# Another written order for the steps of a fused delta-rule and mixer kernel

## The chip, the cores and the metric

The kernel runs on one core of one Trainium2 chip. The metric is the device time of one execution in microseconds (us), lower is better. The kernel before took 581.09, 582.49 and 582.77 us in three runs, so its median is 582.49 us.

The core has five engines, each with its own list of instructions, taken in order: PE (TensorE, the matrix engine; its weight loads are a row of their own, PEld), DVE (VectorE), ACT (ScalarE), POOL (GpSimd) and SP (SyncE, which here only issues DMAs). The program makes the engines wait for each other with semaphores.

## The reference

Two blocks follow each other. The first is a delta-rule recurrence over 4 batches and 8 heads, 768 tokens with head size 48. The second is a mixer on the result with 384 channels: a low-rank mix over the tokens, and then a two-layer channel network of width 1536.

```python
for t in range(S):
    kt, vt, bt = (k_n[:, :, t], v[:, :, t], beta[:, :, t, None])
    y[:, :, t] = np.einsum('bhd,bhde->bhe', q[:, :, t], state)
    v_old = np.einsum('bhde,bhd->bhe', state, kt)
    state = state + bt[:, :, :, None] * np.einsum('bhd,bhe->bhde', kt, vt - v_old)
...
h = xt @ U @ V
u = x + h.transpose(0, 2, 1)
ch = np.maximum(u @ w_ch1, 0.0) @ w_ch2
return (u + ch).astype(np.float32)
```

`k_n` is k divided by its norm, and `xt` is x with tokens and channels exchanged.

## The kernel before

**Work.** The recurrence is done in chunks of 64 tokens, 12 per batch. A batch is cut into two units of six chunks, so there are eight units, n = 0 to 7. For a unit, `grams` transposes k and q (`turn`, line 374) and forms products of keys with keys and of queries with keys (`products`, line 400). `blocks` (line 439) inverts the 32x32 triangles on DVE by forward substitution. For each column it multiplies into `prod` (line 468) and subtracts from `xt` (line 469). That is 15 columns for units 0 to 2, which work on half triangles, and 31 for the others. `joins` (line 501) builds the 64x64 inverses from the triangles by short alternations of PE, ACT and DVE. Then `recur` (line 599) walks the 12 chunks of a batch. For units 0 and 1 a chunk is a PE step that applies the old state (line 697), a DVE step that forms `z` (line 704), a PE step for the new state (line 714) and a DVE step that adds it up as `s` (lines 720 and 722). From unit 2 on there are three PE steps: line 673, then `rest` on DVE (line 679), line 686, then `z` on ACT (line 689), line 714, then `s` on DVE. `outputs` (line 614) computes y of a chunk, and `put` copies it to `X` with ACT.

**Weights.** The weights arrive as 64-bit numbers. `load_weights` (line 748) loads them in 14 slices, and converts each with three DVE steps (lines 809, 815 and 818) and one ACT step (line 796). The 14 slices are U, V, six for the first layer, six for the second.

**Mixer.** A batch has three groups of 256 tokens. `front` (line 1015) does the low-rank mix and the transposition, `channels` (line 1099) the first layer in six pieces, `narrow` (line 1178) the second layer in four. `early` (line 929) and `ahead` (line 944) do the first layer of the very first group from x before its low-rank part is there. They are the first long matmuls of the program. `ahead` needs `early`, which needs the first four chunks of batch 0 in `X`, and the first-layer weights. The last batch takes another way for the first layer (`quick`, line 866).

**Order.** No planner runs in the kernel. Each piece of work is a Python generator, a *part*, which yields one step after another. A step is a few instructions of one engine. Parts get numbers as they begin, and `ORDER` (line 52) is a list of 2342 part numbers. `run` (line 186) walks it and lets the named part emit its next step. A number behind a dot names the PSUM bank, and a q asks for the form of a mixer step that works on quarters of the matrix engine (64x64 tiles). Since each engine has its own list, a token's place matters only against other tokens of the same engine. The parts 0 to 200 begin before the first token, so they have the same numbers in every order, for instance: 4, 9, 10, 11 are `recur` of batches 0 to 3; 12 is `norms` of unit 0; 17 and 18 turn q of unit 0; 19, 34, 51, 68, 85, 102, 119, 136 are `blocks` of units 0 to 7; 23 and 24 load v of unit 0; 146 is `load_weights`, 147 to 160 the loads of its slices; 162 is `weight_sums`; 166 is `early`, 167 to 172 are `ahead`. Parts that begin later (outputs, joins, channels) have numbers that depend on the order.

```python
for token in ORDER.split():
    i, bank, quad = (token.partition('q')[0] + '.').split('.')[0], token.partition('.')[2], 'q' in token
    step = waits[int(i)]
    if isinstance(step, tuple):
        step = step[quad]
```

## Time and profile before

| what | value |
|---|---|
| runs | 581.09, 582.49, 582.77 us; median 582.49 us |
| profiled execution, first to last instruction | 581.3 us |
| PE busy | 549.3 us (94%) |
| DVE busy | 405.2 us (70%) |
| ACT busy | 248.1 us (43%) |
| mean granted PE clock | 0.988 |

The profile is of one execution, and only its span is shown, not its time with what lies around the span. The span stands 1.2 us below the median of the runs and 0.2 us above the fastest of them.

The views used are: the page's busy sums and its rows in 40 slices of 14.5 us; the table of busy time by stretch, in which each row has the stretch, its length, and for every engine busy us and number of instructions, then the granted clock, the DMA share and GB/s; the chain of work that ended last, in order of time (start, us, what); the list of who waited for whom; and the groups of instructions by line. A busy PE means only that matmuls are under way, since they overlap.

### The profile page before, as it was taken

Reading aid. Unit: us, or ns where it says so; the run is one execution under the profiler, and the core shown is the slowest. Engines: PE = TensorE matmul, PEld = TensorE weight load, DVE = VectorE, ACT = ScalarE, POOL = GpSimd, SP = SyncE. Lnnn points to the kernel's source line nnn. Section 1 sums busy time; section 2 is a strip of 40 time slices with the busy share of each in tenths; the row PEclk is TensorE's granted clock in tenths of the full one; section 3 lists DMA queues with packets and bytes.
Section 4 is the critical chain, followed back from the end, with each engine's and each line's share of the span. In section 5 each row is a group of like instructions: output and inputs, shape, how many; then the busy total and the mean of one; then the engine's idle time right before and its main releaser. Section 6 shows DMA issues by size and latency. Waiting matters only on the chain.

```text
span 581.3 us, 25150 instructions
## 1 busy us (share of the span) xinstructions
PE 549.3 (94%) x11349; PEld 464.3 (80%) x11349; DVE 405.2 (70%) x1006; ACT 248.1 (43%) x526; POOL 97.8 (17%) x169
## 2 busy tenths in 40 slices
PE   5766999999999999999999999999999999999997
PEld 4665887669889788789879876989879869656997
DVE  6999875699998239899972899998323248157442
ACT  3678886553333553254245323631531331465000
POOL 8212150260001214221014105200000000000000
PEclk9999689999999999999999999999999999999999
DMA  9997292280000243620014204200000000000010
GB/s 146 171 249 194 75 224 54 56 151 6 30 4 16 46 76 62 111 45 3 30 24 95 61 14 85 54 29 2 31 3 2 31 2 1 28 1 0 15 41 28
DMA packets 63851, 33.38 MB, mean 57 GB/s; under 512 B 50816, under 2 KB 61824, under 8 KB 63744
## 3 DMA queue, kind: packets, MB, share of 16 engines
q1 hardware_dynamic: 56800, 23.21, 18.6%
q0 software_dynamic: 5344, 8.27, 6.6%
q8 instruction: 89, 1.46, 1.1%
q10 hardware_dynamic: 1600, 0.30, 0.3%
q14 instruction: 18, 0.15, 0.1%
HBM read 27.03 MB, written 4.72 MB: 55 GB/s over the span
## 4 chain that ended last, share of the span: by engine, by line
PE 80%; DVE 14%; issue 2%; ACT 1%; DMA 1%; SPq 0%; DVEq 0%; ACTq 0%
PE P L1214 25%; PE P L1126 13%; PE P L206 10%; PE P L904 7%; PE P L407 3%; PE P L951 3%; PE P L218 2%; DVE prod L468 2%; DVE xt L469 2%; PE P L628 2%; PE P L621 2%; PE P L686 2%; PE P L923 1%; PE P L1049 1%; PE P L673 1%
## 5 line engine op out<-in xcount | busy, mean ns | idle before, releaser
L1126 PE MATMUL P<-ut,w_sb 128*128 128x256 f32 x384 | 88.4, 385 | 0.1
L1214 PE MATMUL P<-w_sb,hs 128*128 128x192 f32 x456 | 79.9, 330 | 0.5 <-issue 0.5
L1126 PEld LDWEIGHTS P<-ut,w_sb 128*128 128x128 f32 x384 | 71.3, 190 | 11.1 <-issue 1.2
L1214 PEld LDWEIGHTS P<-w_sb,hs 128*128 128x128 f32 x456 | 74.1, 190 | 2.2 <-issue 1.3
L469 DVE TENSOR_TENSOR xt<-xt,prod 128x112 f32<-128x112 f32 (+21 forms) x200 | 64.6, 323 | 6.9
L468 DVE TENSOR_TENSOR prod<-gs,xt 128x112 f32<-128x112 f32 (+21 forms) x200 | 63.5, 318 | 2.5
L1096 ACT ACTIVATE hs<-P 128x512 f32<-128x512 f32 x48 | 28.7, 597 | 66.9 <-PE P L1126 52.4
L206 PE MATMUL P<-ut,w_sb 64*64 64x256 f32 x768 | 55.9, 383 | 0.9 <-ACT hs L1096 0.6
L1160 DVE TENSOR_TENSOR X<-X,P 128x192 f32<-128x192 f32 x85 | 29.2, 347 | 38.1 <-PE P L1214 35.2
L1214 PE MATMUL P<-w_sb,S 128*128 128x192 f32 x240 | 41.6, 329 | 0.0
L1214 PEld LDWEIGHTS P<-w_sb,S 128*128 128x128 f32 x240 | 39.0, 190 | 0.4
L407 PE MATMUL P<-slot 48*64 48x64 f32 x1536 | 34.6, 244 | 4.0 <-issue 2.0
L611 ACT COPY X<-P 64x192 f32<-64x192 f32 x96 | 30.0, 312 | 15.4 <-PE P L628 13.8
L591 POOL MEMSET slot<- 32x384 f32 x32 | 13.7, 433 | 135.7 <-PE P L562 126.0
L587 ACT COPY slot<-zz 32x384 f32<-32x384 f32 x64 | 32.2, 508 | 10.2 <-DVE zz L473 8.9
L407 PEld LDWEIGHTS P<-slot 48*64 48x64 f32 x1536 | 30.9, 156 | 7.0 <-issue 3.0
L206 PEld LDWEIGHTS P<-ut,w_sb 64*64 64x64 f32 x768 | 27.3, 133 | 9.5 <-issue 2.5
L720 DVE TENSOR_TENSOR s<-s,P 128x192 f32<-128x192 f32 x40 | 14.0, 350 | 29.8 <-PE P L714 25.0
L310 POOL DMA_DIRECT2D slot<-in_q_dram x32 | 20.9, 657 | 80.9 <-DVE prod L468 31.1
L689 ACT COPY z<-P 128x192 f32<-128x192 f32 x36 | 11.4, 318 | 53.2 <-PE P L686 45.9
L310 POOL DMA_DIRECT2D slot<-in_k_dram x44 | 29.0, 667 | 22.2 <-PE P L714 17.3
L889 DVE TENSOR_TENSOR slot<-slot,P 128x384 f32<-128x384 f32 x36 | 19.4, 553 | 19.1 <-PE P L904 18.1
(182 smaller groups left out, 1048.1 us busy)
## 6 DMA issues: line engine op xcount, KB each, us to landing
w_sb<-in_moe_w_ch_dram SPq DMA_DIRECT2D x14, 384.0 KB, 4.3
out_dram<-X SPq DMA_DIRECT2D x22, 192.0 KB, 2.0
slot<-in_k_dram SPq DMA_DIRECT2D x48, 72.0 KB, 4.1
slot<-in_k_dram POOLq DMA_DIRECT2D x44, 72.0 KB, 4.3
slot<-in_q_dram SPq DMA_DIRECT2D x32, 72.0 KB, 4.8
slot<-in_q_dram POOLq DMA_DIRECT2D x32, 72.0 KB, 4.9
slot<-in_v_dram SPq DMA_DIRECT2D x32, 72.0 KB, 3.9
slot<-in_v_dram POOLq DMA_DIRECT2D x32, 72.0 KB, 3.0
```

What stands on the lines that cost most here:

```text
L206: nc.tensor.matmul(to[half(g)], w[half(r), half(g)], x[half(r)], start=start, stop=stop, skip_group_check=True)
L310: queue.dma_start(out=t[half(1 - g if name == 'z' else g), :, to, 0:D], in_=src[b, 4 * g + s, hf * UC * L:(hf + 1) * UC * L, :].rearrange( ...
L407: nc.tensor.matmul(p_g[half(g ^ par * i), par, c], kq[rows, c, j, 0, half(g)], kq[rows, c, j, i, half(g)], start=True, stop=True)
L468: nc.vector.tensor_tensor(out=prod, in0=gb[:, :, j:j + 1, j + 1:].to_broadcast([128, split, m, w]), in1=xb[:, :, 0:m, j:j + 1].to_broadcas ...
L469: nc.vector.tensor_tensor(out=xb[:, :, 0:m, j + 1:], in0=xb[:, :, 0:m, j + 1:], in1=prod, op=ALU.subtract)
L587: nc.scalar.copy(pg[quarter(i), :, at, :, a:a + BK], cut(zc, h)[quarter(i)].rearrange('p r (c j) t -> p r c j t', j=2))
L611: nc.scalar.copy(x[half(c % 2), c // 2, 4 * D * g:4 * D * (g + 1)].rearrange('p (j r d) -> p r j d', r=2, d=D), states(p_y)[half(g)])
L904: nc.tensor.matmul(banks[x], w1_sb[:, 4 * a[0] + e, a[1]] if isinstance(a, tuple) else w1_mixes[a][:, e], tokens(*t) if isinstance(t, tupl ...
L1096: nc.scalar.activation(hs[:, fs[0]:fs[1] + 1:fs[1] - fs[0]], p_f, ACTF.Relu)
L1126: nc.tensor.matmul(p_f[:, x], w(x, t), ut[:, t], start=t == 0, stop=t == KT - 1)
L1160: nc.vector.tensor_tensor(out=to, in0=to, in1=p, op=ALU.add)
L1214: nc.tensor.matmul(to, of[0], of[1], start=of[2], stop=of[3], skip_group_check=True)
```

## The change

The text of `ORDER` is replaced. Nothing else in the file differs. Each part has the same number of tokens as before where its number is fixed (0 to 200), the whole list has 2342 tokens before and after, and 25 tokens carry a q in both. So the same steps are issued on the same engines, in another sequence on each of them. A few rows of the diff, from the beginning, the start of batch 1 and the stretch with the last weight sums:

```diff
-    1 0 1 0 1 0 1 0 2 1 36 147 37 21 150 22 36 152 153 151 149 14.3 37 21 201 2 148 201 37 36 22 36 22 21 15.1
-    20 38 202.2 148 203 39 146 148 146 204 203 2 37 21 146 205.0 202 22 154 148 202 26 38 202 29.3 39 205 149
...
-    223 220 146 34 226 218 27 218 34 218 34 217 146 217 220 217 155 34 155 218.3 218 220 155 34 218 220 217
...
-    326 330 9 330 319 319 9.1 330 9 341.2 342 9.0 9 324 331q 9.1 331 9 341 343.0 331 9.1 341 331 9 324 9.1 341
...
+    1 0 0 0 0 1 14.3 1 1 15.2 147 201 150 202 201 146 204 203.1 203 202 205.0 205 37 37 146 146 203 203 36
+    205 205 2 2 2 2.3 36 2 2 2 36 36 19 20 205 12 29.2 21 206 2 12 19 19 19 37 37 30.3 19 38 38 208 39 39 19
...
+    152 24 151 212 212 34 34 34 156 216 213 213 213 24 214.3 214 214 151 26 26 214.3 214 220 220 34 34 146
...
+    9 9.2 320 68 321 318 318 318 68 291.0 291 291 9 291 68 303 306 306 68 323 9.2 326 326.1 326 9 325 328
...
+    330 9 330 342 326 326 9.0 9 61 9.0 9 331q 331 75 325 331 9.0 9 341 343.2 341 341 325 325 325 331 9.0 9
```

## The prediction

> **What bounds the kernel now.** I read the page first: busy sums and the rows in 40 slices.

> ```profile
> span 581.3 us, 25150 instructions
> ...
> PE 549.3 (94%) x11349; PEld 464.3 (80%) x11349; DVE 405.2 (70%) x1006; ACT 248.1 (43%) x526; POOL 97.8 (17%) x169
> ...
> PE   5766999999999999999999999999999999999997
> ...
> DVE  6999875699998239899972899998323248157442
> ...
> PEclk9999689999999999999999999999999999999999
> ```

> PE is at 9 everywhere but in the first four slices. An order can only win where PE has nothing to do, so I asked for the busy time by stretch, cut where the first long matmuls (`ahead`, line 951) start in the chain of waits, at 77 us. Columns: stretch, length, then busy us of PE, PEld, DVE, ACT, POOL, clock, DMA.

> ```profile
> 0.00:77.00 77.00, 55.05 (x1708) 50.05 (x1712) 66.41 (x188) 54.34 (x104) 25.15 (x46) 0.91 0.78 173
> 77.00:130.00 53.00, 51.21 (x1267) 38.35 (x1256) 38.44 (x82) 32.77 (x62) 20.99 (x34) 1.00 0.56 108
> 130.00:570.00 440.00, 435.06 (x8347) 368.16 (x8347) 298.57 (x733) 160.94 (x361) 51.66 (x89) 1.00 0.15 32
> ```

> PE idles 22.0 us before 77 us, 1.8 us from there to 130, and 4.9 us in the next 440. So there are two regimes: a start of 77 us in which PE is fed late, and then a PE that is full. What feeds it late is in the chain of the start (start us, us, what):

> ```profile
> 41.05 1.04 DVE w_sb L818
> ...
> 63.10 0.24 DVE z L704
> ...
> 66.79 0.37 DVE z L704
> ...
> 77.42 2.35 PE P L951 x10
> ```

> From 12.4 to 67 us nearly every link of this chain is DVE, and in 12 to 66.8 us DVE is busy 51.6 of 54.8 us. The link at 66.79 is z of the fourth chunk of batch 0, the last that `early` needs, and `early` opens `ahead`. So the start lasts as long as the DVE work written before that z. Part of it is weight conversion:

> ```profile
> L818 DVE SCALAR_TENSOR_TENSOR w_sb<-w_sb,X 128x768 uint16<-128x768 uint32 x7 | 7.1, 1019 | 0.0
> L809 DVE TENSOR_SCALAR power<-w_sb 128x768 int32<-128x768 int32 x7 | 4.1, 591 | 0.0
> L815 DVE TENSOR_SCALAR X<-w_sb 128x768 int32<-128x768 int32 x7 | 4.1, 589 | 0.0
> ```

> A full slice costs 1.02 + 0.59 + 0.59 = 2.2 us of DVE, and one ACT cast of 1.06 us (line 796). After 77 us the waits of PE are few and short (waited for; us in total, times, longest):

> ```profile
> PE P L621 <- DVE s L720: 1.0, 3, 0.6
> PE P L1214 <- DVE X L1160: 0.9, 2, 0.4
> ```

> **The change, part by part.** It removes and adds no instruction, so each cost is one of place. I counted tokens of parts with fixed numbers, and told later parts by their pattern of dots and counts; a step's time is its row's busy sum over its count.

> *Start, DVE.* Before, the z in question is the sixth DVE token of part 4, list place 336, and 26 tokens of part 146 (the conversions) stand ahead of it: eight slices and two steps of a ninth. After, it is at place 299 with 17 tokens ahead: five slices and two steps. The same DVE work of units 0 and 1 stands ahead in both: part 19 whole, part 34 whole, both norms, the masks. So 3 x 2.2 = 6.6 us of conversion move behind z, which comes near 60.2 us. The end of blocks 1 (last token of 34) goes from place 302 to 283 with it.

> *Start, other engines.* Ahead of the first token of 167, ACT has 90 tokens instead of 108 (four or five casts of 1.06 us, a dozen copies of 0.5 us, so about 9 us less). ACT was busy 14.2 us of 60 to 75, so it needed this relief, or it would have been the next bound. From z to `early` it took 66.8 to 74.3 us, with PE steps of 6.8 us by their rows in between; now 3.2 us of steps stand there, 3.6 less. From `early` to `ahead` it took 3.1 us with 4.6 us of steps, now 6.8, so about 1.5 more. The first `ahead` matmul moves by -6.6 - 3.6 + 1.5 = -8.7 us, to about 69. Against it: PE has done less by then. Five `joins` steps (0.64 us in the 32x32 form, 0.79 in the other, together 3.5) now stand behind. All PE groups sum to 647 us by their rows against 549 busy, since steps overlap, so this costs 3.0 us later. The moved conversions find room: DVE has 14.6 us free in 77 to 130, and the sixth first-layer slice is still converted ahead of the `ahead` step that uses it.

> *Start, DMAs.* Loads are reordered on SP and POOL. The queries of unit 0 come later (last on SP is its 22nd issue, not its 16th; turned at places 116 and 143 instead of 79 and 106), and v of unit 0 must wait for that turn. Before, v is issued from 23.0 to 28.7 us on SP, is scaled on DVE at 38.05, and lands in 3.9 us (median). After, the last turn stands behind some 24 us of DVE work, and before the z link 62 us of such work ended at 66.8, so about 5 us are to be added: it comes at about 30 us, v lands at about 38, and its scaling, with 41 us of DVE work ahead of it, is due at about 46. That leaves about 8 us, so I cost it at nothing; without that cover each us late is a us lost.

> So the start gives -8.7 + 3.0 = -5.7 us. Bounds: -1, if the alternations of `joins` (PE waits of 4.4 us at lines 525, 539 and 561 in the start) become the chain once fewer conversions stand between them, and -9, if the deferred steps find gaps of PE.

> *After the start, recurrence gaps.* Between two PE steps of a recurrence lies an eviction (0.35 us, rows of lines 720 and 679) and its hand-overs. What hides it is PE work written in between: a y step is 0.47 us (20.9 us over 44), a turn 0.66, a single `ahead` step 0.51, a quarter-array piece 0.87, another recurrence step 0.45. Before, most gaps behind the first `ahead` step hold 0.87 us or more. Five hold less: three in batch 0 and two in batch 1. If 0.9 us is the need, they miss 1.9 us in sum, and the waits of PE after 77 us that name s, z or rest or their ACT copies sum to 1.8. So I take 0.9. After, 13 hold less: four in batch 0 (missing 1.4), six in batch 1 (2.5; in the row `9.0 9 61 9.0` nothing at all stands between), two in batch 2 (0.9) and one in batch 3 (0.4). That is 5.2 instead of 1.9, +3.3 us. Bounds: 0, if the evictions come sooner, and +9, below.

> *After the start, changes of tiling.* A block of 12 narrow matmuls takes 2.15 us alone and 1.95 in a run of 36 (chain), so a change of tiling costs about 0.2 us. From the first `ahead` step on I count 148 instead of 150 changes: -0.4 us.

> *Late weight sums.* The seven tokens of 162 (0.69 us of DVE each) move from places 554 to 900 to places 1575 to 2110. That takes 4.8 us off DVE where it is busy 57 of 60 us (120 to 180), and the last stands shortly ahead of `quick`, where DVE is busy 11.8 of 15 us (480 to 495) and narrow steps of 2.1 us cover it. Nothing; without cover 0.7 us.

> Sum: -5.7 + 3.3 - 0.4 = -2.8 us on the profiled span of 581.3. The median stands 1.2 us above that span; the same step from it gives 582.5 - 2.8 = **579.7 us**.

> **The clock.** The table by 2 us has PE at half clock from 64 to 76 us, while it is busy:

> ```profile
> 64.00:66.00 2.00, 2.00 (x82) 0.50 0.27 66
> 66.00:68.00 2.00, 1.83 (x64) 0.50 0.11 28
> ```

> The sum leaves this stretch as it is. A new order could lose it or lengthen it; at half clock 12 us hold 6 us of full-rate work, the bound on either side. [...]

> **The rivals.**
> 1. *The gaps cost nothing.* Then 582.5 - 5.7 - 0.4 = 576.4. For it: the list of PE waits after 77 us is short in all. Against: the match of 1.9 and 1.8 above.
> 2. *The gaps cost much more; slower.* In 225 to 300 and 330 to 405 us DVE is busy 14 of 15, mostly with columns of `blocks` of about 0.64 us a pair (64.6 + 63.5 us over 200). If each of the eight new short gaps waits for the whole need and one such pair in front, 1.5 us with 0.4 covered, they cost 1.1 each, about 9: 582.5 - 6.1 + 9 = 585.4. It decides from 0.76 us a gap on. For it: nothing written behind a waiting matmul goes ahead of it, and DVE is loaded just there. Against: the old short gaps show at most 0.6.
> 3. *The start moves and nothing is won.* DVE is at 95% from 120 to 180 us too; if work moved behind z comes due there, PE waits for it later: 582.5. Against: the 14.6 us free before, and the weight sums that leave that stretch.
> 4. *The clock.* Half of its bound: 579.7 - 3 = 576.7.

> **Chances.** Forecast 0.44, rival 1 0.18, rival 2 0.22, rival 3 0.10, clock 0.06. The forecast's own range is 577.5 to 581.5. Within 0.3% (1.75 us, about what a measurement of this kernel can tell from no change) lie rival 3 and a fifth of the forecast's 0.44; so faster 0.59, same 0.19, slower 0.22. The range takes in rivals 1 and 2 and some of their spread: 574.5 to 586.

> **What would show it.** Right: the first line-951 matmul at about 69 us, not 77; five full or partial slices (lines 809 to 818) before the fourth chunk's z, and that z near 60 us; PE idle before `ahead` of about 17 us, not 22; PE waits named s, z or rest of some 5 us after it. Wrong: `ahead` as late as before, with PE or DVE waiting for a v load or an ACT copy, waits above 1 us at the short gaps, or DVE waits for weight slices.

## The result, and the profile after

The kernel after took 603.98, 605.17, 606.88 and 609.43 us, median 606.0, against 582.6 (four runs) before: the ratio is 1.039, 95% interval 1.035 to 1.044. The change costs 23 us. Forecast were 579.7 us, a range of 574.5 to 586, and a chance of 0.22 for slower. The profiled execution is the slowest of the four: span 607.7 us, against 581.3 before.

The page after, the same lines as before:

```profile
span 607.7 us, 25161 instructions
...
PE 557.8 (92%) x11349; PEld 471.9 (78%) x11349; DVE 409.5 (67%) x1006; ACT 245.6 (40%) x527; POOL 96.4 (16%) x169
...
PE   5466898999899999899998999999999999999997
...
DVE  6878665789689426899977477989753316556552
...
PEclk9999559999799999999999999999999999999999
```

PE does the same 11349 matmuls. It is busy 8.5 us longer and idles 17.9 us more (49.9 instead of 32.0). The row PEclk, and the clock column of the tables by stretch, count as full clock all the time ahead of the clock's first record, which begins at 57.3 us after and at 59.9 us before; what that hides is told under "The clock" below. The table of busy time by stretch after, cut where the first `ahead` matmul starts and 53 us later, as before (line numbers after are those of before plus 2):

```profile
0.00:83.00 83.00, 52.81 (x1613) 48.23 (x1614) 62.10 (x176) 51.19 (x100) 24.23 (x46) 0.87 0.68 149
83.00:136.00 53.00, 49.22 (x1165) 36.68 (x1166) 36.39 (x77) 29.63 (x55) 14.30 (x24) 0.89 0.53 103
136.00:596.00 460.00, 447.36 (x8524) 378.91 (x8523) 308.92 (x749) 164.76 (x374) 57.91 (x99) 0.99 0.15 33
```

PE idles 30 us in the start, not 22, and 3.8 and 12.6 us in the two other stretches, not 1.8 and 4.9. What it waits for is in the lists of waits of PE (us in total, times, longest), first two lines of before, then the top of the list after, without its first line, the load of the first keys:

```profile
PE P L407 <- issue: 2.0, 2, 1.2
...
PE P L525 <- DVE zz L473: 1.9, 2, 1.5
```

```profile
...
PE P L409 <- ACT slot L397: 5.6, 2, 3.1
PE P L527 <- DVE zz L475: 5.4, 1, 5.4
PE P L650 <- issue: 2.3, 1, 2.3
PE P L716 <- issue: 2.2, 1, 2.2
PE P L527 <- issue: 2.2, 1, 2.2
PE P L575 <- issue: 1.9, 1, 1.9
```

Two kinds of wait have grown. The first two lines after are waits of the start: PE stands at a step whose input is late (in before 2.0 and 1.9 us for the same two). The others are called "issue": PE waits for nothing that this list shows, and it does so in the middle of a group of like matmuls (in before 1.2 us at most). The chain of waits after has two of them in the start:

```profile
57.75 1.71 issue
...
63.39 2.21 issue
...
82.64 1.65 PE P L953 x3
```

The last line is the first `ahead` matmul, at 82.6 us; it was 77.4 before and forecast at 69.

To see where the time goes, I added up PE's matmuls in their order, each with the mean time of its line in the trace of before. This gives a moment for the same amount of PE work in both traces, the "curve of equal PE work". After stands behind before by 7.8 us at 42 us, 7.5 at 73, 11.2 at 95, 15.5 at 113, 15 until 157, 19.8 at 176, 20 to 21 until 325, 24.4 at 343, 26.6 at 375, and 26.4 at the end. So most of it is lost in the start, soon after it, and then in two steps of 4 to 5 us whose places are those of the "issue" waits at 158 and 332 us.

### The profile page after: what moved, and what is told of

It reads as the page before. It is cut to its first block, busy times and chain, and to the rows that moved or that the text cites. A ratio compares the mean times of both kernels' runs of the same rounds, so it can differ in the third digit from the quotient of the medians.

```text
span 607.7 us, 25161 instructions
## 1 busy us (share of the span) xinstructions
PE 557.8 (92%) x11349; PEld 471.9 (78%) x11349; DVE 409.5 (67%) x1006; ACT 245.6 (40%) x527; POOL 96.4 (16%) x169
## 3 DMA queue, kind: packets, MB, share of 16 engines
q8 instruction: 89, 1.46, 1.0%
## 4 chain that ended last, share of the span: by engine, by line
PE 78%; DVE 11%; ACT 5%; issue 4%; DMA 1%; SPq 0%; DVEq 0%; ACTq 0%
PE P L1216 23%; PE P L1128 14%; PE P L208 10%; PE P L906 6%; PE P L409 3%; PE P L953 3%; DVE xt L471 2%; PE P L623 2%; PE P L716 2%; PE P L688 2%; DVE prod L470 2%; PE P L675 2%; PE P L630 2%; PE P L220 2%; PE P L541 1%
## 5 line engine op out<-in xcount | busy, mean ns | idle before, releaser
L1216 PE MATMUL P<-w_sb,hs 128*128 128x192 f32 x456 | 83.9, 342 | 1.1 <-DVE xt L471 1.1
L1216 PEld LDWEIGHTS P<-w_sb,hs 128*128 128x128 f32 x456 | 78.4, 199 | 4.1 <-issue 1.6
L471 DVE TENSOR_TENSOR xt<-xt,prod 128x112 f32<-128x112 f32 (+21 forms) x200 | 64.6, 323 | 6.9
L208 PE MATMUL P<-ut,w_sb 64*64 64x256 f32 x768 | 51.5, 382 | 0.1
L312 POOL DMA_DIRECT2D slot<-in_k_dram x44 | 28.7, 658 | 68.7 <-PE P L716 68.0
L397 ACT COPY slot<-P 128x768 f32<-128x768 f32 x30 | 23.5, 804 | 22.9 <-PE P L220 22.5
L312 POOL DMA_DIRECT2D slot<-in_v_dram x32 | 20.8, 655 | 69.1 <-PE P L220 69.0
L1216 PE MATMUL P<-w_sb,slot 128*128 128x192 f32 x180 | 30.4, 327 | 0.9 <-DVE X L1162 0.9
L1216 PEld LDWEIGHTS P<-w_sb,slot 128*128 128x128 f32 x180 | 29.3, 190 | 1.7 <-DVE X L1162 1.5
```

The source lines that it names most:

```text
L208: nc.tensor.matmul(to[half(g)], w[half(r), half(g)], x[half(r)], start=start, stop=stop, skip_group_check=True)
L312: queue.dma_start(out=t[half(1 - g if name == 'z' else g), :, to, 0:D], in_=src[b, 4 * g + s, hf * UC * L:(hf + 1) * UC * L, :].rearrange( ...
L471: nc.vector.tensor_tensor(out=xb[:, :, 0:m, j + 1:], in0=xb[:, :, 0:m, j + 1:], in1=prod, op=ALU.subtract)
L1216: nc.tensor.matmul(to, of[0], of[1], start=of[2], stop=of[3], skip_group_check=True)
```

## The experiments

Changes in us are ratio minus one, times 583 us, where no other base is named.

### Which part of the order costs how much

Since every order issues the same steps, the first part of one can be joined to the rest of the other: the first part is issued, then all steps not yet issued in the sequence of the other order. PSUM banks are given anew along the whole list; what other banks cost by themselves was not measured.

**The start of before, the rest of after** (cut at the first `ahead` step; the beginning of the list, against after):

```diff
-    1 0 0 0 0 1 14.3 1 1 15.2 147 201 150 202 201 146 204 203.1 203 202 205.0 205 37 37 146 146
+    1 0 1 0 1 0 1 0 2 1 36 147 37 21 150 22 36 152 153 151 149 14.3 37 21 201 2
...
```

> The written order of before up to its first step of ahead, and from there all remaining steps in the sequence of after. Theory A (the loss of 23.4 us is made in two places: about 11 us up to the first 95 us, where the curve of equal PE work stands 11.2 us behind, and the rest in stretches of small matmuls after that): about 606 - 11 = 595 us, 591 to 599. Theory B (all of it follows from the start, whose delay is only handed on): 583 to 586. Theory C (all of it is in the later order, the start costs nothing): 603 to 607. The stalls of PE in the middle of a group that stand at 158 and 332 us in after (2.2 and 1.9 us) should be there under A and C.

**The start of after, the rest of before** (the beginning of the list, against before):

```diff
-    1 0 1 0 1 0 1 0 2 1 36 147 37 21 150 22 36 152 153 151 149 14.3 37 21 201 2
+    1 0 0 0 0 1 14.3 1 1 15.1 147 201 150 202 201 146 204 203.2 203 202 205.0 205 37 37 146 146
...
```

> The written order of after up to its first step of ahead, and from there all remaining steps in the sequence of before. Theory A (start and rest each cost about half): 582.6 + 8 to 11, so 590 to 594. Theory B (all of it in the start): 603 to 607. Theory C (all of it in the later order): 582 to 584. If the two halves add up, the two mixed kernels together stand 23 us above twice the time before.

Measured: 1.021 (1.013 to 1.029), 12.4 us, and 1.020 (1.015 to 1.026), 11.9 us. (Of the first, one execution took 1798 us, with its matmuls about three times as long. It is left out; it is also the one that was profiled, so no trace shows this kernel at its usual speed.) Each half costs about 12 us, give or take 3 to 5, and they add up to the 23: theory A. The "issue" waits at 158 and 332 us are gone from the trace of the kernel whose rest is that of before.

### What the "issue" waits are

The page has a queue that loads instructions, q8: 89 packets, 1.46 MB, so 16.4 KB a packet. PE has 22,816 recorded instructions before (weight loads, matmuls, waits) and 22,828 after, so a packet is 256 of them. I counted PE's records up to each gap of 0.35 us or more. The "issue" waits above lie at record 193 or 194 modulo 256, which makes that the border of a block. All gaps at such a border or at most nine records from it are, with their us and the moment they begin:

```
before          0.89@16.8 1.18@25.3 0.70@54.2 0.81@117.2 0.36@145.2 0.52@375.4                  sum  4.5
after           0.45@44.6 1.71@57.8 2.21@63.4 2.30@101.3 2.18@158.1 0.53@211.5 1.15@253.6
                1.94@331.7 0.59@433.7 0.36@490.7                                                sum 13.4
before shifted  4.17@14.4 1.16@25.4 0.86@49.6 1.23@65.6 3.54@90.9 1.03@118.8 1.22@161.7
                0.55@212.3 2.99@243.3 0.87@350.3 1.73@390.5                                     sum 19.4
```

Six of them the lists of waits put down to another engine, ACT or DVE: 0.89 and 0.70 in before, 0.53 and 1.15 in after, 1.16 and 0.86 in before shifted.

**The cost by itself.** 512 matmuls of 32x32 tiles at the very beginning, each of which is two matmuls and two weight loads in the trace, so 2048 instructions:

```diff
     with tc.manual_schedule():
+        for i in range(512):
+            nc.tensor.matmul(P[quarter(i % 4), 7, 384:416], ident[quarter(0), quarter(i % 4)], ident[quarter(0), 0:BK], start=True, stop=True)
```

> Before, with 512 matmuls of 32x32 tiles (2048 instructions of PE) at the very beginning, where nothing else uses PE: the cost in dispute by itself. Theory F: they run in bursts with a stop at every 256 instructions, some 3.4 to 3.5 us from burst to burst, so about 28 us for all eight blocks. Rival (no limit on the supply): an even pace, set by the matmuls alone.

The timeline of PE in this kernel (start us, length, line, matmuls in a run, then the idle time before the run and what ended it):

```profile
3.24 3.22 PE L1236 MATMUL P<-ident 32*32 32x32 f32 x223 [3.24 <-DVE P L252]
10.36 1.93 PE L1236 MATMUL P<-ident 32*32 32x32 f32 x128 [3.90 <-issue]
17.65 1.93 PE L1236 MATMUL P<-ident 32*32 32x32 f32 x128 [5.36 <-issue]
26.59 1.93 PE L1236 MATMUL P<-ident 32*32 32x32 f32 x128 [7.01 <-issue]
30.04 1.93 PE L1236 MATMUL P<-ident 32*32 32x32 f32 x128 [1.53 <-issue]
33.77 1.93 PE L1236 MATMUL P<-ident 32*32 32x32 f32 x128 [1.80 <-issue]
...
```

The first 223 matmuls run without a stop, which was not expected. Behind them each run is 128 matmuls with 128 weight loads: 256 instructions, 1.93 us of work. The runs start 3.45 to 3.73 us apart from 26.6 us on, where the DMA engines are nearly idle (share 0.02). Earlier, while the first loads are on their way, they start 7.3 and 8.9 us apart, so that all of it takes 38 us and not 28. The kernel took 618.7 us in its one run, 35 us more.

The packets of q8 are in the trace too, with their times, and they show what PE waits for. (In this kernel there are 97 instead of 89, so 8 more for 2048 more instructions.) From 26.6 us on, the packet for the next block starts 1.04 to 1.23 us after PE has begun a block, takes 0.9 to 1.2 us, and PE goes on 1.24 to 1.51 us after its end. Earlier the packet starts 4.1 and 6.2 us after, with the DMA engines at a share of 1.20 and 1.11 in between. In after, PE goes on 1.2 to 1.7 us after the end of such a packet at all five "issue" waits above, and in the traces of eight of these kernels 43 of the 44 stops of 0.9 us or more at a border end 1.2 to 1.8 us after one (the other is a wait for DVE). So PE does stop for its instructions: a block took 3.45 us at best in these runs of small matmuls, and 7.3 and 8.9 us where loads occupied the DMA engines (shares of 1.20 and 1.11). As a strict limit 3.46 us does not hold: from one record 193 to the next single blocks take less, 3.30 us from 430.9 us in after with a stop of 0.59, 2.99 from 442.8 without one, and 3.29 from 44.9 in before. The packets of q8 start no closer than 3.31 us in after and 3.36 in before.

**The same order, shifted borders.** 32 transposes of the identity at the beginning, where PE waits for the first keys, let every later border fall 64 instructions earlier in the order. (They cost nothing by themselves: the second `turn` of PE starts at 12.5 us with them, and at 12.8 in before.)

```diff
     with tc.manual_schedule():
+        for _ in range(32):
+            nc.tensor.transpose(P[:, 7, 384:512], ident, ident)
```

> The order of before, with 32 extra transposes of the identity (64 instructions of PE) at the very beginning, where PE waits for the first keys. They cost no time of their own. Theory F (PE gets its instructions in blocks of 256, a block cannot be used up in less than some 3.46 us, the shortest seen in the trace of after, and so the time depends on where the borders of the blocks fall in the order): with the pace of PE in the trace of before, borders 64 instructions earlier leave 7.2 us of such stalls instead of 0.6, so 588 to 592 us, and the stalls stand 64 instructions earlier in the program than in before, near 85, 107, 228, 331 and 370 us. Rival (the issue waits have to do with the instructions themselves, not with a border): 582 to 584 and the same stalls as before.

> The order of after, with the same 32 transposes at the beginning as before_shifted_64 had. With the pace of PE in the trace of after, borders 64 instructions earlier leave 12.0 us of stalls in blocks below 3.46 us, instead of 6.6 where they are. Theory F, if that holds: 611 to 618. If before was only lucky with its borders, and any shift of after is as good as where it is: 602 to 608.

Before shifted: ratio 1.027 (1.022 to 1.032), 15.6 us, with no step of the order moved. Its stops (the third row above) are again at record 193 or 194 modulo 256, now 64 instructions earlier in the order. The five worked out for 85, 107, 228, 331 and 370 us are there, at 91, 119, 243, 350 and 391, later by the delay that adds up. The size was underestimated: 588 to 592 us were expected, 600 came. The stops of 3.54 and 2.99 us at 91 and 243 us fall where loads run (DMA shares of 1.34 from 90 us and 1.18 from 243), and the table by stretch shows the first of them (columns as before):

```profile
90.00:92.00 2.00, 0.89 (x70) 0.74 (x62) 0.55 (x2) 1.56 (x2) 0.57 (x1) 1.00 1.34 240
92.00:94.00 2.00, 0.00 (x0) 0.00 (x0) 1.97 (x4) 0.00 (x0) 0.00 (x0) 0.84 0.63 97
94.00:96.00 2.00, 1.56 (x12) 1.31 (x12) 0.28 (x1) 0.96 (x2) 0.00 (x0) 0.50 0.01 2
```

The DMA share is 1.34 when PE's block should come, PE does nothing from 92 to 94, and then runs at half clock until 100. After shifted: 611.8 us, ratio to before 1.049 (1.044 to 1.055), against 1.039 for after: 5.8 us more, where 5.4 were worked out. The same working gave 6.6 for before, where 15.6 were measured, so that it fits here is luck in part.

So the time of before owes something to where its borders fall. With the pace of PE in its trace, what its blocks lack to 3.46 us sums to 0.6 us where the borders are, and to 1.0 to 9.2 at 15 other positions 16 instructions apart. For after it is 6.6 where they are, and 4.2 to 13.4 elsewhere. (These sums leave out blocks that come late because of loads, and the half clock behind a stop, so the measured loss is larger.)

**Runs of small matmuls broken up.** The order of after has eight `joins` steps back to back at 330 us, which start within 1.7 us; each has 24 matmuls and as many weight loads, so they are 384 instructions. Five PE steps of long matmuls were written a little earlier, into four such runs; once in after, once in the mixed kernel with the start of before. Excerpts of the list:

```diff
-    7.0 7.1 7 146 146 170 170
+    7.0 170 170 7.1 7 146 146
...
-    289 291.1 291 69 61 61 289 270
+    289 270 291.1 291 69 61 61 289
...
-    437 440.1 435 440 121 124 124 124 437 121 438.2 121 438 435 438 110 420
+    437 420 440.1 435 440 121 124 124 124 437 121 438.2 121 438 435 438 110
```

> The order of after with five PE steps of long matmuls written a little earlier, into four runs of small matmuls: two ahead steps between the two prepare steps at 100 us, a narrow step in front of the last two joins steps at 157 us, a narrow step in front of the front step at 251 us, a narrow step into the middle of eight joins steps at 330 us. Theory F (a block of 256 PE instructions cannot be used up in under 3.46 us, and the stall then takes the clock down for some us): the stalls of 2.3, 2.2, 1.2 and 1.9 us at 101, 158, 254 and 332 us shrink to under 0.6 each, 6 us, and the half-clock stretches behind them go, 2 to 4 us more: 606 - 8 to 10, 595 to 599. Rival (the stalls are no more than where PE waits for something that comes late anyway): 603 to 608, with the same time lost in waits of another name.

> The order of before up to ahead, then that of after with the same runs of small matmuls broken up. If start and stalls add: 596 - 8 to 10 = 586 to 588. If the stalls in the rest are what is left of its loss (596 - 584 = 12): down to 584. Rival (the rest of after loses by its short recurrence gaps, not by the stalls): 592 to 597.

After broken up: 1.033 (1.026 to 1.039) instead of 1.039 (1.035 to 1.044), 4 us; the intervals overlap, and 601.9 us misses the 595 to 599 expected. With the start of before: 1.008 (1.005 to 1.010) instead of 1.021 (1.013 to 1.029), 8 us, clear of noise and as expected. Why the first gained less is not shown. In its profiled execution `ahead` starts 1.6 us later than in after (84.3 and 82.6 us), though nothing ahead of it was moved. The stops at 158, 254 and 332 us are gone from the trace of after broken up; the one at 101 us has become two, 0.87 at 104 and 1.49 at 108 us, so that edit won nothing. The table by stretch at the second place, first after, then broken up:

```profile
156.00:158.00 2.00, 2.00 (x193) 1.77 (x191) 2.00 (x8) 0.00 (x0) 0.00 (x0) 1.00 0.11 24
158.00:160.00 2.00, 0.11 (x13) 0.01 (x1) 1.79 (x8) 1.90 (x4) 0.00 (x0) 0.91 0.03 8
160.00:162.00 2.00, 1.71 (x6) 1.67 (x7) 0.83 (x1) 0.13 (x1) 0.00 (x0) 0.50 0.03 8
```

```profile
156.00:158.00 2.00, 2.00 (x104) 1.75 (x103) 2.00 (x6) 0.00 (x0) 0.00 (x0) 1.00 0.16 43
158.00:160.00 2.00, 2.00 (x51) 1.77 (x52) 1.79 (x8) 1.52 (x3) 0.00 (x0) 1.00 0.03 8
```

After issues 193 matmuls in 2 us, stands for the next 2 and goes on at half clock; broken up there is neither the stop nor the fall. So of the 12 us that the rest of the order costs, about 8 are these stops with the half clock behind them, by the clearer of the two tests, and 4 are left.

### What the start costs, and why

Two more mixed kernels, with the rest broken up. The first is cut at the first `joins` step of before, place 145 (the list around the cut, against before):

```diff
-    212.1 19 215 213 150 19 212 218 218.3 35 212 221 218 212 213 26 212 34 43 218 33.2 221
+    212.3 19 215 213 150 19 212 218 212 220 212 212 34 146 212 212 218.3 218 222 221 221 221
```

> The order of before for its first 31 us (to its first joins step), then all remaining steps in the sequence of after, with the runs of small matmuls broken up. Beside after_runs_broken_up (601.9) and before_start_rest_broken_up (587.2) it divides the start's loss. Theory H (the curve of equal PE work stands 7.8 us behind at 42 us because the products of the keys of unit 1 are written ahead of the q turns and hold PSUM banks until DVE comes to them): 594 to 595, and v of unit 0 issued at about 23 us. Rival (what is won by 42 us is lost again by 77, where PE takes its instructions at its limit in either order): 599 to 603. Rival (all of the start's loss is made before 31 us): 586 to 589.

The second is cut at the first recurrence step, place 276:

```diff
-    5 34 5 219 219 229 220.2 41 4.1 41 220 4 34 230.3 220 4.0 34 220 231.1 4 230 6.2
+    5 34 5 219 219 229 220.0 41 156 220 220 220 6.0 4.1 4 4.3 231.2 6.1 6 34 4 4.0
```

> The order of before up to the first recurrence step of PE (which starts at 54.9 us), then all remaining steps in the sequence of after, with the runs of small matmuls broken up. It lies between before_until_31_rest_broken_up (602.1) and before_start_rest_broken_up (587.2), so it tells in which part of the order the 15 us between these two are made. If it is the joins and prepare steps of unit 0 (31 to 55 us): 587 to 591. If it is the late conversions and their ACT steps (after 55 us), which alone cost before 6.7 us: 594 to 598. If it is all behind 55 us: 600 to 603.

Measured: 1.031 (1.024 to 1.037), or 602.1 us, and 1.020 (1.015 to 1.025), or 595.8; with no start of before it was 601.9, with all of it 587.2. Each of these is known to 2 to 4 us. So the first 31 us of the order show no gain, though v of unit 0 is issued at 23.2 us there, and at 36.9 in after. The steps from 31 to 55 us are worth about 6 us, those from 55 us to `ahead` about 8.5, either give or take 3 to 5. Theory H, that the late q turns make the loss, falls.

**The first step of the prediction by itself.** Before, with its conversions (part 146) and the ACT casts behind them moved behind z of the fourth chunk, as far as after has them there; the list of PE is unchanged:

```diff
-    220 146 5.0 34 146 146 5 34 5 219 219 229 220.2 41 4.1 41 220 4 34 230.3 220 4.0 34 220
+    220 5.0 34 5 34 5 219 219 220.2 41 4.1 41 220 4 34 229.3 220 4.0 34 220
...
```

> Before, with one part of the change alone: nine conversion steps of DVE and the ACT steps that follow them moved behind z of the fourth chunk, as after has them. The list of PE is that of before. Theory of the prediction (the start lasts as long as the DVE work ahead of that z): z at about 60 to 61 us instead of 66.8, the first ahead matmul near 70, total 576 to 579. Rival D (z is soon held by the alternation of PE, ACT and DVE in joins and in the recurrence, so only part of the 6.6 us is won): z at 63 to 65, total 580 to 582. Rival E (the conversions then come due at ahead, which waits for weights): 583 to 586.

Measured: 1.011 (1.006 to 1.016), 6.5 us slower; 590.9 us is above what all three theories expected. z of the fourth chunk starts at 66.95 us; before it was 66.79. DVE's list ahead of it is shorter (46.3 us busy from 12 us to z, before 51.6), but DVE now waits. The top of its list of waits from 12 to 67 us:

```profile
DVE s L721 <- PE P L715: 3.3, 2, 1.9
DVE z L705 <- PE P L698: 1.3, 1, 1.3
```

What it waits for is PE; in the same list of before no wait of DVE for PE appears. In before PE uses five blocks between 44.9 and 66.4 us, 21.5 us for what at 3.46 us a block is 17.3, and has no stop for instructions at a border. Here it has stops of 1.30, 0.64, 0.58, 1.65 and 1.48 us at the borders between 48 and 68 us, 5.7 in sum. The moved conversions did not bring these stops: the kernel with the start of before and the rest broken up has the DVE list of before up to `ahead`, and its trace has stops of 1.38, 0.83, 1.06 and 1.79 us at four of the same borders, with z at 66.24 us. There DVE has conversions to do while PE stands, and here it has none. Why the profiled execution of before has no such stops, no run shows. The conversions then come all at once, and ACT stands behind them. The timeline of ACT:

```profile
...
83.95 1.06 ACT L797 CAST w_sb<-power 128x768 f16<-128x768 f32 x1 [1.05 <-DVE power L810]
85.03 0.32 ACT L612 COPY X<-P 64x192 f32<-64x192 f32 x1
```

This cast, like the one at 79.4 us, waits for its conversion, with an output copy (line 612) behind it that PE waits 3.2 us for. `ahead` starts at 85.9 us instead of 77.3.

**Is z held by PE's list?** Four `joins` steps of unit 1 (192 instructions) moved behind the fourth chunk's first PE step, with late conversions and in before as it is:

```diff
-    236 236.3 52 231 4 238 234 234.1 238 4.0 41 146 234 239 236 146 43 238 239 4 146 239 4.0
+    236 52 231 4 238 234 238 4.0 41 146 239 146 43 238 239 4 146 239 4.0 236.3 234.1 234 236
```

> Before with the nine conversions moved behind z of the fourth chunk (as in before_conversions_late), and on PE also the first two joins steps of each half of unit 1 (four steps of 48 instructions) moved from ahead of the fourth chunk's first PE step to behind it. Theory F (between 45 and 66 us PE is at the pace at which it gets instructions, five blocks of 256 at 3.5 us, so that z comes as late as PE's list before it is long): z of the fourth chunk at 64 to 65 instead of 66.95. Theory of the prediction (DVE's list sets it): z where it was, 66.5 to 67. The total stays at 588 to 593 in either case, since the conversions still come late.

> Before, with only those four joins steps of PE moved behind the first PE step of the fourth chunk; all other lists as before. Theory F: z of the fourth chunk 1 to 2 us sooner than 66.8 (DVE has four conversion steps, 2.9 us, between 63.4 and 66.6, which now lie in its way), the total 581 to 585. Theory of the prediction: z at 66.8 and the total as before, 582 to 584, or later by what the joins lose, 584 to 587.

z came at 66.15 and 66.83 us, the times were 1.012 (1.007 to 1.016) and 0.998 (0.996 to 1.000). So the simple form of theory F falls here: 192 instructions fewer in front gain 0.8 us with the conversions out of the way, and nothing without. In the first of these traces a stop of 1.71 us at 57.3 holds the second chunk's `s` to 59.7 us, the transposition of blocks 1 on DVE (2.0 us) follows it, and a stop of 1.12 us at 63.3 lies in the next recurrence step. The way to z alternates between PE, its instructions and DVE, and the relief of one uncovers the next.

**PE and ACT steps of the start in another sequence.** In after, PE waits 5.4 us at a `joins` step (line 527) from 24.7 us on. The q turns, a product and two ACT copies were written ahead of it:

```diff
-    3 209 207 216 209 209 34 211 146 21 207 17.2 219 39 39 149 149 3 22 209 209 3 3 214.3
+    3 209 17.2 218 207 216 209 209 34 211 146 21 207 39 39 149 149 3 22 209 209 3 3 18.0 33.1
...
```

> The order of after with the first q turn, its ACT copy, the two other q turns of units 0 and 1, one product step and one more ACT copy written ahead of the first joins step of PE (which waits 5.4 us for the first joins transposition of DVE), instead of behind it. Theory H (the start of after is lost because PE and ACT stand at a step that waits, with work behind it that could run): the wait of 5.4 us at 24.7 us shrinks to under 3, v of unit 0 is issued some 4 us sooner, and 3 to 5 us of the start's loss go: 601 to 603.5. Rival (the start is set by the pace at which PE gets its instructions, five blocks of 256 between 45 and 66 us, and by the DMAs, so the idle time only moves): 604.5 to 608.

Measured: 1.035 (1.030 to 1.040) against 1.039 (1.035 to 1.044): the intervals overlap, so the time does not decide. The trace speaks against theory H: v of unit 0 is issued at 36.6 us, not 4 us sooner than the 36.9 of after. The wait has moved rather than shrunk, as the list of waits of PE says: the next turn now waits, from 25.4 to 33.3 us, for an ACT copy that stands behind DVE's columns of blocks 0 and empties the PSUM bank that the turn is given.

```profile
PE P L220 <- ACT slot L420: 7.9, 1, 7.9
```

**`early` sooner.** Before, with the first five `joins` steps of unit 1 and their ACT copies behind the copies of the fourth chunk's output, and `early` ahead of them:

```diff
-    231 236 236.3 52 231 4 238 234 234.1 238 4.0 41 146 234 239 236
...
+    231 236 52 231 4 234 4.0 41 146 146 43 4 146 4.0 237 146
...
```

> Before, with the first five joins steps of unit 1 and their ACT copies written behind the copies of the fourth chunk's output, and early directly behind those copies, ahead of the joins. If the way from z to the first ahead matmul (66.8 to 77.3 us) is made by the ACT copies of joins that stand between, ahead comes 2 to 4 us sooner and the total is 579 to 582. Rival (PE then waits at early with the joins behind it, and ahead waits for the PSUM banks that joins hold): 584 to 590.

Measured: 1.014 (1.009 to 1.018). `early` came at 70.6 us instead of 74.2, and `ahead` at 85.3 instead of 77.3: the rival, and more than its 584 to 590 (592.5). No version beat before; moving only the four `joins` steps of unit 1 cannot be told from it.

## Why the prediction was wrong

**The start, -5.7 us; measured about +12.** The counts were right: five slices and two steps of conversion stand ahead of the fourth z after. The step that failed is "the start lasts as long as the DVE work written before that z". DVE was busy nearly all the time up to z, so I took its list for the bound. From 12 us to z it was busy 51.6 of 54.8 us before and 47.5 of 60.2 after: its list got shorter and z came later, at 72.2 us, not 60. Its list of waits from 12 us to z after, of which none for PE is in that of before, says for what:

```profile
DVE s L722 <- PE P L716: 3.8, 1, 3.8
...
DVE s L724 <- PE P L716: 1.2, 1, 1.2
```

PE's stop of 2.21 us at 63.4 lies within the wait of 3.8 us. The test alone (conversions late) shows it without the rest of the change: z stayed where it was. PE with its instructions was nearly as much of a bound (21.5 us for five blocks that at 3.46 us each are 17.3), and a busy sum does not show that: a PE that runs 256 small matmul instructions in 1.93 us and waits 1.53 us for the next, as in the kernel with the 512 matmuls, looks half idle.

**"The moved conversions find room."** They do in the sum (14.6 us of DVE free) but not in time: they come due together ahead of `ahead`, and hold ACT's queue. Alone this costs 6.5 us. This is rival 3's mechanism (moved work comes due where it is waited for), at a higher price. I had given it no more than the loss of the gain.

**Loads and q turns, nothing.** v was issued later than worked out (36.9 us, not 30), and the cover still held: undoing the first 31 us of the order, v included, moved the time by 0.2 us, with each time known to some 4 us.

**Short gaps, +3.3 us; about +1.** Waits of PE that name s, z or rest after `ahead` sum to 2.8 us, before to 1.8. None is above 0.5. That is nearer to rival 1 than to the forecast, and rival 2 is out.

**Changes of tiling, -0.4 us, and late weight sums, nothing.** The first is too small to be seen here. For the second, the sums run at 369 us and between 451 and 522 us, and the curve of equal work is flat from 375 us on.

**The clock.** I took PE to be at half clock from 64 to 76 us alone, as the row PEclk and the table by 2 us draw it. That reading was wrong, since both count the time ahead of the first record as full. In before shifted the 32 transposes start 0.21 us apart until 8.0 us and 0.11 us apart from there, and its first record, of full clock, begins at 8.0. And the matmuls of line 407 take 311 ns (median) ahead of the first record of before and 218 at full clock behind it; in after (line 409) those at recorded half clock take 311. So the start runs at half clock, but for one stretch of 3.4 us: in before until 77.0 us, just ahead of the first `ahead` matmul, and in after until 91.4, 8.8 us behind it, and again for 3 to 7 us behind the stops at 101, 158 and 332 us. In after 17 matmuls of `ahead` and 28 of `narrow` run at half clock. By the mean time from one start to the next, at half and at full clock, that costs about 8 us (3.5 and 4.5), an estimate from this one execution; in before it is nothing, and in after broken up 3.0. It is nearly all of the 8.5 us that PE is busy longer. My sum left the clock as it was, and 8 us is beyond the bound of 6 that I gave it.

In after, stops of 2.2 us at 158 and 1.9 us at 332 were followed by half clock, while a stop of 1.0 us at 119 in before shifted was not, nor were stops of 2.49, 1.87 and 2.10 us at 98, 157 and 248 in after shifted. So the length of the stop alone does not decide it, and what does was not shown. The mean clock of an execution counts the time without record as full, and does not tell its time: executions of after with 0.997 had spans of 603.5 and 605.1 us, one with 0.972 had 602.3, and one with 0.963 had 607.7.

**What was missing.** No case of mine held that the order decides how PE's instructions are spread over the blocks. The sign for it was in the profile of before, in waits named "issue" in the middle of a group, 0.8 us at line 407. The 23 us divide into about 12 for the start, of which 6.5 are what the late conversions cost alone, about 8 for the stops behind the start with the half clock behind them, and 4 that no run here explains. What the steps from 31 to 55 us cost in detail (about 6 us) stays open too; a `joins` step that waits ahead of other PE work is argued, not shown.

## What to carry to other kernels

Count the instructions of a matmul engine as well as its time: runs of small matmuls that held 256 instructions in less than some 3.5 us stopped at the block border here (1.5 us in the kernel with the 512 matmuls, 2.2 us at 158 us in after), and a long step written into the run took the stop away at three of four places. 64 instructions added at the beginning moved the later borders by 64, and that alone cost these two orders 2.7% and 1.0%; shift the borders once on purpose to see how much of a difference is that. And before a busy engine is called the bound, relieve it alone: what it waits for then is the next bound. And check a clock row against the duration of like matmuls before it is read as full.

## What the runs showed that was not expected

In the kernel with the 512 matmuls a block of 256 PE instructions took 3.45 us at best, for 1.93 us of work, and 7.3 and 8.9 us while the DMA engines were fully used (shares of 1.20 and 1.11); PE went on 1.2 to 1.8 us after the packet with its instructions had ended. 64 instructions more at the start of a program, with no cost of their own, made it 2.7% slower. The clock fell to half 1.5 us after a stop of 2.2 us began (at 158 us after), and stayed there for 6.8 us; after a stop of 2.49 us (at 98 us after shifted) it did not fall. And the start, which the profile draws at full clock, ran at half: its matmuls of line 407 took 311 ns, against 218 later.
